# First head pair of a fused attention and two-layer kernel: keys and queries kept whole in float32, bias rows multiplied apart, half of these rows on GpSimd's queue

## The chip, the core and the metric

One core of a Trainium2 chip runs the whole program. The metric is the device time of one execution in microseconds (us), as the median of the runs; lower is better. The core's engines run side by side, each through its own queue in order: TensorE (PE, with its weight loads shown apart as PEld), VectorE (DVE), ScalarE (ACT), GpSimd (POOL) and SyncE (SP), which only issues transfers.

## What is computed

Attention over 4 batches of 8 heads, 576 positions and 64 values a head, with a bias made of running sums, and then two feed-forward layers over all 2304 tokens. Cut to what matters here:

```python
scores = scale * np.matmul(q, k.transpose(0, 1, 3, 2))        # scale = 1/8
cum = np.cumsum(np.maximum(s, 0.0), axis=-1)
bias = -(cum[:, :, :, None] - cum[:, :, None, :])
scores = np.where(causal, -1e9, scores + np.minimum(bias, 0.0))
attn = exp(scores - max(scores)); attn = attn / sum(attn)
x = attn @ v                                                   # then
x = gelu_like(x @ w_in) @ w_out                                # layer 1
out = rational(x @ w2_in) @ w2_out                             # layer 2
```

## The kernel before

Heads go in pairs, four pairs to a batch, sixteen in all. A pair has five **units**, tiles of 128 query rows taken in the order t = 0, 1, 4, 2, 3 (unit 4 holds the last 64 rows of both heads). A unit's scores are made per head h over the n keys that the causal mask leaves: `s_0_2_1` is batch-0 pair 0, unit 2, head 1. In the names of the program's order the last number is only a counter.

**How float32 accuracy is made.** PE takes reduced-precision `float32r` operands in one pass. `prep` turns the keys and queries of a head by PE transposes into PSUM (`tk`, `tq`; `turn`), then splits them: ACT writes a rounded high part (`hi`, L213), DVE writes the rest (`lo`, L216), two ops each of 64 x 288 for a head's keys and as many for its queries. The high parts are then doubled onto the other 64 partitions (`move`; for the first two pairs by GpSimd casts, L251). So a score is two matmuls into one PSUM tile (`scores_piece`, L289): one on 68 partitions (`k2`: low keys with high queries, and in partitions 64 to 67 four **bias rows**, running sums against ones), one on all 128 (`kh`, `qs`).

**Where the bias rows come from.** `sums` makes the running sums in two column parts, `PARTS` = 0 to 256 and 256 to 576 (DVE scan L118), `sum_parts` splits each part into high and low (ACT L129, DVE L130) in the buffer that the trace calls `stgA`, and `open_rows` has SP move them into `k2` (L136): eight transfers for pair 0 (two parts, two heads, two sides), four for pair 1. SP's next transfer after pair 0's eight is the first of the raw weights (L547).

**The loop.** Each step j of `attention` issues the scores of unit j for head 0, then the transposes of the unit three steps back (`tp`, L381; L360 for unit 4), then head 1's scores, then values of older units (`O`, L406). DVE reduces a score tile with its mask and finds the row minimum (L319), ACT takes the exponent (L326), DVE inverts the row sums, GpSimd scales the rows (L339). PE follows the written order; the other engines' order is set by a scheduler. While there is nothing else for PE to do, in the first five steps, `fill` and `warm` put idle bf16 matmuls of 512 columns (L82) between the others: they compute nothing that is used. From step 4 on, ACT, DVE and POOL also convert raw weights (L558 to L567). From the second batch on, layer 1's matmuls of an earlier batch (L638, L662) fill PE's gaps.

Of the kernel before, what the change touches and what calls it, by code (L numbers as in the profile page):

```python
# [10 lines left out]
F32 = mybir.dt.float32  # L11
F32R = mybir.dt.float32r
# [3 lines left out]
AF = mybir.ActivationFunctionType  # L16
ALU = mybir.AluOpType
# [8 lines left out]
NB, NH, S, D = 4, 8, 576, 64  # L26
# [3 lines left out]
P = 128  # L30
# [18 lines left out]
PARTS = ((0, 256), (256, 576))  # L49
ZEROS = 5  # L50
WARM = 6
RUN_ENDS = ((0, 1, 4, 2, 3), (3,), (3,), (3,))
W2_SLOTS = 7
LEAD = 2
# [7 lines left out]
class Fused:  # L62
# [70 lines left out]
    def sum_rows(self, g, src, h=slice(0, 2), c=slice(0, S)):  # L133
        d = self.k2[g % 2][D : D + 4].bitcast(F32)
        for i in range(2):
            self.moved = self.nc.sync.dma_start(d[2 - 2 * i : 4 - 2 * i, i, h, c], src)  # L136

    def open_rows(self, g):
        for c0, c1 in ((0, S),) if g else PARTS:
# [59 lines left out]
    def prep(self, att, b, p, ld, first=False):  # L199
        nc, ident = self.nc, self.ident  # L200
        h0, h1 = slice(0, D), slice(D, P)

        def new(nm):
            return att.tile([P, 2, S], F32R, name=f"{nm}{b}_{p}", tag=nm, bufs=2)

        g = b * NP + p
        kh, qs, k2 = new("kh"), new("qs"), self.k2[g % 2]
        self.pairs[b, p] = {"kh": kh, "qs": qs, "k2": k2, "ld": ld, "O": None}  # L210

        def hi(out, T, scale):
            self.parts[0] = nc.scalar.activation(out, T, AF.Copy, scale=scale)  # L213
# [7 lines left out]
        def turn(nm, h):  # L221
            T = self.bank("T", f"t{nm}{b}_{p}_{h}")
            x = ld[nm][:, h].rearrange("i t d -> i (t d)")
            for t in range(3):
                nc.tensor.transpose(  # L225
                    T[:, t * R6 : (t + 1) * R6], x[:, t * P : (t + 1) * P], ident[:R6, :R6]
                )
            return nm, T[:, : 3 * R6].rearrange("p (t i) -> p i t", i=R6), h

        def split(*parts):  # L230
# [10 lines left out]
            for i, (high, low, T, scale) in enumerate(jobs):  # L241
                with self.behind((self.parts[1],) if i else ()):
                    lo(low, T, high, scale)

        def main(nm):
            split(*[turn(nm, h) for h in range(2)])

        def move(o, i, hs=(0, 1)):
            if g < 2:
                for h in hs:  # L250
                    self.copied = nc.gpsimd.tensor_copy(o[:, h], i[:, h].bitcast(F32))  # L251
            else:
                nc.sync.dma_start(o.bitcast(F32), i.bitcast(F32))

        if first:
            turned = [[turn(nm, h) for nm in "kq"] for h in range(2)]
            for h in range(2):
                with self.behind(first):
                    split(*turned[h])
                first = tuple(self.parts)  # L260
                if h == 0:
                    with self.behind(first):
                        first = self.sum_parts(PARTS[1])
                move(kh[h1], kh[h0], (h,))
                move(k2[h0, 1], qs[h0], (h,))
            self.warm(WARM)
            return
        if g > 1:
            self.sum_rows(g, self.rows[g])
        main("k")  # L270
        move(kh[h1], kh[h0])
        yield
        main("q")
        move(k2[h0, 1], qs[h0])
        yield


# [1 line left out]
    def scores_piece(self, u, sc, hs, j0, w):  # L279
        nc = self.nc  # L280
        b, p, t = u
        pr = self.pairs[b, p]
        for h in hs:
            c0, c1 = t * P, (t + 1) * P
            if t == 4:
                c0, c1 = (S - P if h else S - 64), S
            k2 = pr["k2"][: D + 4]
            for m, (q, k) in enumerate(((k2[:, 1, h], k2[:, 0, h]), (pr["qs"][:, h], pr["kh"][:, h]))):
                nc.tensor.matmul(  # L289
                    sc[: c1 - c0, :w], lhsT=q[:, c0:c1], rhs=k[:, j0 : j0 + w],  # L290
                    start=m == 0, stop=m == 1,
                )

    def unit_scores(self, att, u, h):
# [12 lines left out]
        if t == 4:  # L307
            sc = self.bank("S", f"s{b}_{p}_{t}_{h}")
            j0, w = 288 * h, 288
            self.scores_piece(u, sc, (1, 0), j0, w)  # L310
            mask = self.mask[:, 0:288] if h == 0 else self.mask[:, 640:928]
            i = h
        else:
            sc = self.bank("S", f"s{b}_{p}_{t}_{h}")
            self.scores_piece(u, sc, (h,), 0, max(n, 256))
            j0, w = 0, n
            mask = self.mask[:, 640 - n : 640]
            i = 0
# [17 lines left out]
        rc = nc.vector.reciprocal(inv[:, c], inv[:, c])  # L336
        self.tail = (ex, rc)
        for i, bt in enumerate(bts):
            nc.gpsimd.tensor_scalar(bt[:, :n], bt[:, :n], inv[:, i : i + 1], 1.0, ALU.mult, ALU.mult)  # L339

    def unit_transpose(self, att, u):
        nc, ident = self.nc, self.ident
# [90 lines left out]
    def attention(self, att, mlp):  # L433
# [24 lines left out]
            with self.behind((self.moved,)):  # L458
                self.store_sums()
        opened = self.moved  # L460
        with self.behind((self.copied,)):
            loads[2] = self.pair_load(att, 0, 2, eng=nc.gpsimd)
        later.extend(loads[i]["values"] for i in (1, 2))
        for j in range(n + AHEAD + 1):
            i, k = j - AHEAD, j - AHEAD - 1
            self.zeros = j < ZEROS
# [25 lines left out]
            self.fill(q / 3, j < 4)  # L492
            for _ in tr:
                pass
            if j < n and idx == 4:
                for _ in nprep:
                    pass
                g = b * NP + p
                g = {0: 3, 1: 4, 2: NB * NP}.get(g, g + 2)
                if g < NB * NP:  # L500
                    with self.behind((opened,)):
                        loads[g] = self.pair_load(att, *divmod(g, NP))
                    later.append(loads[g]["values"])
# [506 lines left out]
```

## Time and profile before

| | us |
|---|---|
| median of 3 runs (1021.01, 1022.94, 1023.03) | 1022.94 |
| the profiled execution | 1021.61 |
| its span, first instruction to last | 1019.6 |
| PE busy | 998.2 (98%) |
| DVE, ACT, POOL busy | 797.3, 718.2, 337.8 |

The profiled execution is 2.0 us longer than its span and 1.3 us shorter than the median. Busy shares are means over stages: the opening (about 25 us), the rest of the first batch (to about 90 us), the other three batches (to about 300 us) and the two layers have different limits. In the rows below, a time is us from the start of the span, and the bracket at a row's end is the idle time of its engine just before it, with what ended it.

### The profile page before, as it was taken

Reading aid. Unit: us, or ns where it says so; the run is one execution under the profiler, and the core shown is the slowest. Engines: PE = TensorE matmul, PEld = TensorE weight load, DVE = VectorE, ACT = ScalarE, POOL = GpSimd, SP = SyncE. Lnnn points to the kernel's source line nnn. Section 1 sums busy time; section 2 is a strip of 40 time slices with the busy share of each in tenths; the row PEclk is TensorE's granted clock in tenths of the full one; section 3 lists DMA queues with packets and bytes.
Section 4 is the critical chain, followed back from the end, with each engine's and each line's share of the span. In section 5 each row is a group of like instructions: output and inputs, shape, how many; then the busy total and the mean of one; then the engine's idle time right before and its main releaser. Section 6 shows DMA issues by size and latency. Waiting matters only on the chain.

```text
span 1019.6 us, 19822 instructions
## 1 busy us (share of the span) xinstructions
PE 998.2 (98%) x7053; PEld 933.9 (92%) x7054; DVE 797.3 (78%) x1804; ACT 718.2 (70%) x1661; POOL 337.8 (33%) x503
## 2 busy tenths in 40 slices
PE   7889999999999999999999999999999999999997
PEld 4679999999999999999999999999999999989996
DVE  7897666766537977777778747998988989889886
ACT  5999889878756655555555436787887777777775
POOL 5778656554410012222111112232222222222222
PEclk9999999999999999999999999999999999999999
DMA  7664564543237546776666644010010100100000
GB/s 180 157 175 100 135 188 146 152 123 72 59 125 247 177 140 196 230 235 224 212 189 235 208 133 190 1 31 32 3 60 1 32 32 1 63 1 1 32 1 32
DMA packets 79074, 115.97 MB, mean 114 GB/s; under 512 B 25552, under 2 KB 63072, under 8 KB 77440
## 3 DMA queue, kind: packets, MB, share of 16 engines
q1 hardware_dynamic: 72640, 94.94, 31.4%
q0 software_dynamic: 6112, 19.47, 5.1%
q8 instruction: 56, 0.92, 0.4%
q14 instruction: 42, 0.34, 0.1%
q10 hardware_dynamic: 224, 0.30, 0.1%
HBM read 74.78 MB, written 31.60 MB: 104 GB/s over the span
## 4 chain that ended last, share of the span: by engine, by line
PE 89%; DVE 4%; DMA 3%; ACT 2%; issue 1%; POOL 0%; SPq 0%; ACTq 0%; DVEq 0%
PE h L638 38%; PE a L815 19%; PE a L662 19%; PE s L289 5%; PE O L406 4%; PE tp L381 3%; DMA raw<-in_moe_w_in_dram 1%; DVE bt L319 1%; DMA x2p<-st 1%; DVE k L216 1%; PE tq L225 1%; PE tk L225 1%; ACT bt L326 0%; PE tp L360 0%; DVE qs L216 0%
## 5 line engine op out<-in xcount | busy, mean ns | idle before, releaser
L638 PE MATMUL h<-x,u 128*128 128x288 f32 x1536 | 231.5, 296 | 1.2 <-ACT st L677 1.2
L662 PE MATMUL a<-gh,u 128*128 128x288 f32 x1024 | 231.7, 297 | 0.0
L638 PEld LDWEIGHTS h<-x,u 128*128 128x128 f32 x1536 | 212.8, 188 | 3.1 <-ACT st L677 1.5
L798 POOL TENSOR_TENSOR gl<-u,gh 128x384 fp32r<-128x384 f32 x96 | 105.7, 1101 | 290.4 <-ACT gh L796 266.4
L662 PEld LDWEIGHTS a<-gh,u 128*128 128x128 f32 x1024 | 173.0, 188 | 1.1 <-issue 0.5
L638 PE MATMUL h<-y,u 128*128 128x384 f32 x864 | 165.7, 336 | 0.0
L638 PEld LDWEIGHTS h<-y,u 128*128 128x128 f32 x864 | 152.9, 188 | 6.2
L662 PE MATMUL a<-gl,u 128*128 128x288 f32 x512 | 150.0, 295 | 0.7 <-DVE gl L655 0.7
L815 PE MATMUL a<-u,gh 128*128 128x512 f32 x432 | 114.6, 394 | 0.9 <-ACT gh L796 0.9
L649 ACT ACTIVATE g<-h 128x288 f32<-128x288 f32 x128 | 52.0, 407 | 75.8 <-PE h L638 75.4
L724 POOL DMA_DIRECT2D x<-xp x64 | 35.3, 552 | 207.3 <-DVE g L650 106.7
L662 PEld LDWEIGHTS a<-gl,u 128*128 128x128 f32 x512 | 96.5, 188 | 1.4 <-DVE gl L655 0.9
L326 ACT ACTIVATE bt<-bt,mn 128x128 f32<-128x128 f32 (+2 forms) x144 | 84.1, 585 | 19.3 <-DVE mn L319 18.2
L815 PEld LDWEIGHTS a<-u,gh 128*128 128x128 f32 x432 | 80.0, 188 | 14.9 <-ACT gh L796 1.8
L339 POOL TENSOR_SCALAR bt<-bt,sm 128x128 f32<-128x128 f32 (+2 forms) x144 | 81.7, 579 | 30.0 <-DVE sm L336 21.6
L796 ACT ACTIVATE gh<-u 128x384 fp32r<-128x384 f32 x96 | 50.6, 527 | 57.6 <-DVE u L794 56.6
L319 DVE CUSTOM_DVE_ANT_0 bt<-s,mask 128x128 f32<-128x128 f32 (+2 forms) x144 | 68.9, 482 | 27.6 <-PE s L289 25.5
L652 ACT ACTIVATE gh<-g 128x288 fp32r<-128x288 f32 x128 | 56.5, 442 | 45.6 <-DVE g L650 43.8
L650 DVE SCALAR_TENSOR_TENSOR g<-g,h 128x288 f32<-128x288 f32 x128 | 57.5, 450 | 29.8 <-ACT g L649 29.2
L781 ACT ACTIVATE y<-h,cf 128x384 f32<-128x384 f32 x96 | 55.4, 577 | 33.9 <-PE h L638 33.9
L786 DVE SCALAR_TENSOR_TENSOR y<-s,cf,y 128x384 f32<-128x384 f32 x96 | 59.3, 618 | 20.6 <-ACT s L783 19.3
L794 DVE SCALAR_TENSOR_TENSOR u<-y,u 128x384 f32<-128x384 f32 x96 | 73.5, 765 | 1.1
(116 smaller groups left out, 2048.0 us busy)
## 6 DMA issues: line engine op xcount, KB each, us to landing
raw<-in_moe_w_in_dram SPq DMA_DIRECT2D x24, 512.0 KB
raw<-in_moe_w_out_dram SPq DMA_DIRECT2D x24, 512.0 KB
x<-xp POOLq DMA_DIRECT2D x64, 144.0 KB, 3.0
wd<-park POOLq DMA_DIRECT2D x36, 256.0 KB, 4.3
u<-wd SPq DMA_DIRECT2D x8, 1024.0 KB
x2p<-st SPq DMA_DIRECT2D x32, 144.0 KB
xp<-x2p SPq DMA_DIRECT2D x32, 144.0 KB
xp<-x SPq DMA_DIRECT2D x32, 144.0 KB
```

What stands on the lines that cost most here:

```text
L319: nc.vector.tensor_tensor_reduce(bt[:, j0 : j0 + w], sc[:, :w], mask, 1.0, 3.0e38 if i == 0 else mn[:, 0:1], ALU.add, ALU.min, mn[:, i : i ...
L326: ex = nc.scalar.activation(bt[:, :n], bt[:, :n], AF.Exp, bias=mn[:, i : i + 1], scale=-1.0, accum_out=sm[:, col : col + 1],)
L339: nc.gpsimd.tensor_scalar(bt[:, :n], bt[:, :n], inv[:, i : i + 1], 1.0, ALU.mult, ALU.mult)
L638: nc.tensor.matmul(ps_tile, lhsT=u[:, wl, kk * P : (kk + 1) * P], rhs=x(xl, kk), start=(n == 0), stop=(n == 3 * KD - 1),)
L650: nc.vector.scalar_tensor_tensor(g[:, :w], g[:, :w], 1.0, h, ALU.add, ALU.mult)
L652: self.newest["act"] = nc.scalar.activation(gh[:, :w], g[:, :w], AF.Copy)
L662: nc.tensor.matmul(acc, lhsT=u[:, wl, d * P : (d + 1) * P], rhs=g[gl], start=(first and i == 0), stop=(last and i == 2),)
L781: nc.scalar.activation(y, h, AF.Abs, scale=cf[:, 4:5])
L786: nc.vector.scalar_tensor_tensor(y, s, cf[:, 7:8], y, ALU.mult, ALU.add)
L794: last = nc.vector.scalar_tensor_tensor(p, y, 2.0, p, ALU.subtract, ALU.mult)
L798: nc.gpsimd.tensor_tensor(gl, p, gh.bitcast(F32), ALU.subtract)
L815: nc.tensor.matmul(accs[m], lhsT=g[gl][:, m * P : (m + 1) * P], rhs=u[:, wl, :], start=(f == 0 and i == 0), stop=(f == NF - 1 and i == 2),)
```

## The change

For pair 0 alone (`PLAIN = 1`):

- keys and queries aren't split. `keep` copies them whole, as float32, onto partitions 0 to 63: head 0's keys and queries and head 1's queries by ACT, head 1's keys by DVE. The low parts and the GpSimd doublings of this pair are gone.
- a score is a float32 matmul on 64 partitions and, after it, a `float32r` matmul on partitions 64 to 67 with the bias rows alone. Unit 0 takes its own 128 columns and not 256.
- head 1's four bias-row transfers go to GpSimd's queue, head 0's four stay on SP's.
- the load of pair 2's keys and queries, on GpSimd's queue too, is issued after the first unit's rows are scaled and not ahead of the loop.

```diff
     def sum_rows(self, g, src, h=slice(0, 2), c=slice(0, S)):
         for i in range(2):
-            self.moved = self.nc.sync.dma_start(d[2 - 2 * i : 4 - 2 * i, i, h, c], src)
+            if g == 0 and h == 1:
+                self.nc.gpsimd.dma_start(d[2 - 2 * i : 4 - 2 * i, i, h, c], src)
+            else:
+                self.moved = self.nc.sync.dma_start(d[2 - 2 * i : 4 - 2 * i, i, h, c], src)
...
+        def keep(engs, *parts):
+            done = []
+            for o in range(2):
+                for nm, T, h in parts:
+                    out = (kh if nm == "k" else qs)[h0, h]
+                    out = out.rearrange("p (i t o) -> p o i t", t=3, o=2)[:, o]
+                    src = T[o * D : (o + 1) * D]
+                    scale = 1.0 if nm == "k" else -0.125
+                    if engs[nm] == "act":
+                        done.append(nc.scalar.activation(out, src, AF.Copy, scale=scale))
+                    else:
+                        done.append(nc.vector.tensor_scalar(out, src, scale, None, ALU.mult))
+            return tuple(done)
...
         if first:
             turned = [[turn(nm, h) for nm in "kq"] for h in range(2)]
-            for h in range(2):
-                with self.behind(first):
-                    split(*turned[h])
-                first = tuple(self.parts)
-                if h == 0:
-                    with self.behind(first):
-                        first = self.sum_parts(PARTS[1])
-                move(kh[h1], kh[h0], (h,))
-                move(k2[h0, 1], qs[h0], (h,))
+            opened = keep({"k": "act", "q": "act"}, *turned[0])
+            with self.behind((*opened, *first)):
+                keys = keep({"k": "dve"}, turned[1][0])
+                with self.behind(keys):
+                    opened = self.sum_parts(PARTS[1])
+            with self.behind(opened):
+                keep({"q": "act"}, turned[1][1])
...
-            for m, (q, k) in enumerate(((k2[:, 1, h], k2[:, 0, h]), (pr["qs"][:, h], pr["kh"][:, h]))):
+            terms = ((k2[:, 1, h], k2[:, 0, h]), (qs, kh))
+            if pr["plain"]:
+                terms = ((qs[:D], kh[:D]), (k2[D:, 1, h], k2[D:, 0, h]))
+            for m, (q, k) in enumerate(terms):
...
-            self.scores_piece(u, sc, (h,), 0, max(n, 256))
+            self.scores_piece(u, sc, (h,), 0, n if self.pairs[b, p]["plain"] else max(n, 256))
...
-        with self.behind((self.copied,)):
-            loads[2] = self.pair_load(att, 0, 2, eng=nc.gpsimd)
...
+            if j == 0:
+                with self.behind((self.normed,)):
+                    loads[2] = self.pair_load(att, 0, 2, eng=nc.gpsimd)
```

PE's order keeps its length. At unit 4's head pass and what stands around it (`s_0_4` scores of unit 4, `tq_1` the query transposes of pair 1, `idle` the fillers, `k_0` the tile `k2` with the bias rows), before:

```order
L82 MATMUL idle<-mask 128x512
L289 MATMUL s_0_4_0_285<-k_0_134 128x288
L289 MATMUL s_0_4_0_285<-kh_0_150,qs_0_151 128x288
L289 MATMUL s_0_4_0_285<-k_0_134 64x288
L289 MATMUL s_0_4_0_285<-kh_0_150,qs_0_151 64x288
L225 MATMUL tq_1_0_291<-ident,spare 128x96 x3
```

and PE's order at the same place now:

```order
L83 MATMUL idle<-mask 128x512
L316 MATMUL s_0_4_0_273<-kh_0_150,qs_0_151 128x288
L316 MATMUL s_0_4_0_273<-k_0_134 128x288
L316 MATMUL s_0_4_0_273<-kh_0_150,qs_0_151 64x288
L316 MATMUL s_0_4_0_273<-k_0_134 64x288
L231 MATMUL tq_1_0_279<-ident,spare 128x96 x3
```

The two matmuls of a piece have changed places, the first is now float32 on 64 partitions and the second has four partitions; the fillers and transposes stand where they stood.

DVE's order in the opening, from the second part of the running sums (L118) to the first score reduction (L319), before:

```order
L118 SCALAR_TENSOR_TENSOR cum<-s_114,cum,nz 32x320
L216 SCALAR_TENSOR_TENSOR k_0_134<-tk_0_0_152,kh_0_150 64x288
L216 SCALAR_TENSOR_TENSOR qs_0_151<-tq_0_0_156,qs_0_151 64x288
...
L130 TENSOR_TENSOR stgA<-cum,stgA 32x320
L216 SCALAR_TENSOR_TENSOR k_0_134<-tk_0_1_160,kh_0_150 64x288
L216 SCALAR_TENSOR_TENSOR qs_0_151<-tq_0_1_164,qs_0_151 64x288
...
L319 ISA bt_0_0_0_216,mn_0_0_0_217<-s_0_0_0_218,mask 128x128
```

and DVE's order there now:

```order
L119 SCALAR_TENSOR_TENSOR cum<-s_114,cum,nz 32x320
L262 TENSOR_SCALAR kh_0_150<-tk_0_1_160 64x288 x2
L131 TENSOR_TENSOR stgA<-cum,stgA 32x320
L346 ISA bt_0_0_0_200,mn_0_0_0_201<-s_0_0_0_202,mask 128x128
```

Eight low parts (four on either side of the sums' second part) have become two copies, and the first reduction follows the sums directly.

GpSimd's order after its masks, before:

```order
L251 CAST kh_0_150<-kh_0_150 64x576
L251 CAST k_0_134<-qs_0_151 64x576
L251 CAST kh_0_150<-kh_0_150 64x576
L251 CAST k_0_134<-qs_0_151 64x576
L181 DMA kn_2_211<-in_k_dram 96x2x384
L181 DMA qn_2_213<-in_q_dram 96x2x384
L339 TENSOR_SCALAR bt_0_0_0_216<-bt_0_0_0_216,sm_0_0_215 128x128
```

and GpSimd's order there now:

```order
L138 DMA k_0_134<-stgA 2x1x256 x2
L138 DMA k_0_134<-stgA 2x1x320 x2
L366 TENSOR_SCALAR bt_0_0_0_200<-bt_0_0_0_200,sm_0_0_199 128x128
L366 TENSOR_SCALAR bt_0_0_1_211<-bt_0_0_1_211,sm_0_0_199 128x128
L185 DMA kn_2_223<-in_k_dram 96x2x384
L185 DMA qn_2_225<-in_q_dram 96x2x384
```

Four casts are replaced by four small transfers, and the load for pair 2 stands behind the first unit's scaling. On ACT, six copies take the place of eight. Further on in the first batch the scheduler has moved some of ACT's and POOL's weight conversions by one to three places.

## Rows read from the trace of the kernel before

**Rows 1.** Busy time by stretch: stretch, its length, busy us (instructions) of each engine, clock.

```profile
16.00:21.70 5.70, 5.67 (x35) 4.10 (x36) 5.03 (x17) 2.95 (x9) 3.09 (x6) 1.00 0.70 152
...
25.00:90.00 65.00, 58.10 (x543) 47.13 (x540) 58.24 (x196) 63.79 (x182) 49.62 (x77) 1.00 0.62 160
90.00:300.00 210.00, 209.06 (x2058) 201.99 (x2057) 129.50 (x441) 169.60 (x486) 112.15 (x198) 1.00 0.42 113
```

**Rows 2.** Chain that ended last, in the opening: start, us, what.

```profile
11.94 3.96 DMA k<-stgA
```

**Rows 3.** Timeline of the opening: start, us, engine, line, operation, out<-in.

```profile
9.16 0.95 DVE L130 TENSOR_TENSOR stgA<-cum,stgA 32x320 fp32r<-32x320 f32 x1
...
9.83 0.81 POOL L251 CAST k<-qs 64x576 fp32r<-64x576 f32 x1
...
11.55 0.46 DVE L216 SCALAR_TENSOR_TENSOR qs<-tq,qs 64x288 fp32r<-64x288 f32 x1
...
12.05 0.29 DVE L319 CUSTOM_DVE_ANT_0 bt<-s,mask 128x128 f32<-128x128 f32 x1
```

**Rows 4.** Timeline of the opening, PE's matmuls.

```profile
9.29 0.36 PE L289 MATMUL s<-k 68*128 68x256 f32 x1 [1.02 <-DMA k<-stgA]
...
16.24 0.29 PE L289 MATMUL s<-kh,qs 128*128 128x288 f32 x1
...
16.37 0.30 PE L289 MATMUL s<-k 68*64 68x288 f32 x1
...
16.64 0.66 PE L225 MATMUL tq<-ident,spare 96*128 96x96 f32 x6
...
17.91 0.61 PE L82 MATMUL idle<-mask 128*128 128x512 bf16 x2
...
18.71 0.39 PE L82 MATMUL idle<-mask 128*128 128x512 bf16 x1
...
20.66 0.60 PE L381 MATMUL tp<-ident,bt 128*128 128x128 f32 x4
...
21.34 0.40 PE L289 MATMUL s<-kh,qs 128*128 128x512 f32 x1
```

**Rows 5.** PE's groups by shape over the whole run: count, busy us, mean ns.

```profile
L406 PE MATMUL O<-pt,vn 128*64 128x128 f32 x640 | 43.3, 277 | 0.0
L289 PE MATMUL s<-kh,qs 128*128 128x512 f32 x32 | 12.8, 400 | 0.0
L406 PE MATMUL O<-pt,vn 128*64 128x64 f32 x320 | 12.2, 223 | 0.0
L289 PE MATMUL s<-kh,qs 128*128 128x288 f32 x32 | 9.5, 297 | 0.0
```

**Rows 6.** Timeline of PE around one block of float32 value matmuls.

```profile
150.23 0.34 PE L289 MATMUL s<-kh,qs 128*128 128x384 f32 x1
150.50 2.99 PE L406 MATMUL O<-pt,vn 128*64 128x128 f32 x60
153.42 0.50 PE L289 MATMUL s<-k 68*128 68x512 f32 x1
```

**Rows 7.** Timeline where the opening ends: DVE's and ACT's last steps for unit 3.

```profile
23.18 0.67 DVE L319 CUSTOM_DVE_ANT_0 bt<-s,mask 128x512 f32<-128x512 f32 x1
...
24.14 0.72 ACT L326 ACTIVATE bt<-bt,mn 128x512 f32<-128x512 f32 x1
...
24.86 0.66 ACT L558 ACTIVATE stgA<-stgA 128x512 int32<-128x512 uint32 x1
```

**Rows 8.** Transfers: two timeline rows, and one of issues with us to landing.

```profile
6.00 6.50 SPq L136 DMA_DIRECT2D k<-stgA  x8
...
10.59 0.84 POOL L181 DMA_DIRECT2D kn<-in_k_dram  x1
...
kn<-in_k_dram POOLq DMA_DIRECT2D x1, 288.0 KB, 3.9
```

More of the change, by code (lines that the diff above doesn't have):

```diff
@@ L51 @@
 WARM = 6
+PLAIN = 1
 RUN_ENDS = ((0, 1, 4, 2, 3), (3,), (3,), (3,))
@@ L201, in prep @@
         h0, h1 = slice(0, D), slice(D, P)
+        g = b * NP + p
+        plain = g < PLAIN
         def new(nm):
-            return att.tile([P, 2, S], F32R, name=f"{nm}{b}_{p}", tag=nm, bufs=2)
-        g = b * NP + p
+            return att.tile(
+                [P, 2, S], F32 if plain else F32R, name=f"{nm}{b}_{p}", tag=nm, bufs=2
+            )
         kh, qs, k2 = new("kh"), new("qs"), self.k2[g % 2]
-        self.pairs[b, p] = {"kh": kh, "qs": qs, "k2": k2, "ld": ld, "O": None}
+        self.pairs[b, p] = {"kh": kh, "qs": qs, "k2": k2, "ld": ld, "O": None, "plain": plain}
         def hi(out, T, scale):
@@ L243, in split @@
                     lo(low, T, high, scale)
-        def main(nm):
-            split(*[turn(nm, h) for h in range(2)])
+        def keep(engs, *parts):
[11 more added lines that the diff above has]
+            return tuple(done)
+        def main(nm):
+            parts = [turn(nm, h) for h in range(2)]
+            if plain:
+                keep({"k": "act", "q": "dve"}, *parts)
+            else:
+                split(*parts)
         def move(o, i, hs=(0, 1)):
@@ L250, in move @@
                 for h in hs:
-                    self.copied = nc.gpsimd.tensor_copy(o[:, h], i[:, h].bitcast(F32))
+                    nc.gpsimd.tensor_copy(o[:, h], i[:, h].bitcast(F32))
             else:
@@ L270, in prep @@
         main("k")
-        move(kh[h1], kh[h0])
+        if not plain:
+            move(kh[h1], kh[h0])
         yield
         main("q")
-        move(k2[h0, 1], qs[h0])
+        if not plain:
+            move(k2[h0, 1], qs[h0])
         yield
@@ L286, in scores_piece @@
                 c0, c1 = (S - P if h else S - 64), S
[L287 to L288 removed]
+            k2, qs, kh = pr["k2"][: D + 4], pr["qs"][:, h], pr["kh"][:, h]
+            terms = ((k2[:, 1, h], k2[:, 0, h]), (qs, kh))
+            if pr["plain"]:
+                terms = ((qs[:D], kh[:D]), (k2[D:, 1, h], k2[D:, 0, h]))
+            for m, (q, k) in enumerate(terms):
                 nc.tensor.matmul(
@@ L338, in unit_scores @@
         for i, bt in enumerate(bts):
-            nc.gpsimd.tensor_scalar(bt[:, :n], bt[:, :n], inv[:, i : i + 1], 1.0, ALU.mult, ALU.mult)
+            self.normed = nc.gpsimd.tensor_scalar(
+                bt[:, :n], bt[:, :n], inv[:, i : i + 1], 1.0, ALU.mult, ALU.mult
+            )
     def unit_transpose(self, att, u):
@@ L460, in attention @@
         opened = self.moved
-        with self.behind((self.copied,)):
-            loads[2] = self.pair_load(att, 0, 2, eng=nc.gpsimd)
-        later.extend(loads[i]["values"] for i in (1, 2))
+        later.append(loads[1]["values"])
         for j in range(n + AHEAD + 1):
@@ L494, in attention @@
                 pass
+            if j == 0:
+                with self.behind((self.normed,)):
+                    loads[2] = self.pair_load(att, 0, 2, eng=nc.gpsimd)
+                later.append(loads[2]["values"])
             if j < n and idx == 4:
```

## The prediction

> **What bounds the kernel now.** I began with the busy time by stretch. From 90 us on PE is busy for 209.06 of 210.00 us, and behind that its work is fixed, so a shift of the moment at which that stretch begins is carried to the end one for one. Ahead of it, from 25 to 90 us, ACT is the fullest engine, 63.79 of 65.00 us [rows 1]: it has 1.21 us of idle time, so a later start there can win back 1.21 us at most. Its work in this stretch isn't touched by the change (pair 0 is split before it; the scheduler only swaps neighbours). So the question is when ACT comes to the end of the opening. I take as marker the last exponent of pair 0's unit 3, which starts at 24.14, right ahead of the first weight conversion at 24.86; it follows DVE's last reduction of pair 0, at 23.18 [rows 7].
>
> What holds the opening before? Not PE: its last score matmul of pair 0 ends at 21.34 + 0.40 = 21.74 [rows 4], 1.4 us ahead of the reduction that reads it. It is DVE and a transfer. DVE writes low parts until 11.55 + 0.46 = 12.01 and only then, at 12.05, reduces its first tile [rows 3]. And the sums' second part, from 9.16, is ready only at 10.11 [rows 3], behind four low parts, so that the last bias rows, issued at 11.94, land at 15.90 [rows 2]; unit 4's scores wait for them. Yet in the stretch from 16.00 to 21.70 PE is busy for 5.67 of 5.70 us [rows 1], fillers included. PE has no room where the change gives it more to do. That decides the case.
>
> **What is removed.** DVE has two copies in place of eight low parts of some 0.46 us: 6 x 0.46 = 2.8 us less. It reaches the sums' second part two steps earlier, at about 8.2, and ends it by 9.2 at the latest (0.95 for that op, during part of which GpSimd's casts run [rows 3]; the casts are gone). ACT has six copies for eight; GpSimd loses four casts, the last from 9.83. All of this lies ahead of the first score or beside it. The first score's gate stays: PE waited until 9.29 for head 0's bias rows [rows 4], and the two transfers that bring them still go out first on SP, from 6.00 [rows 8]. What is late next is PE.
>
> **What PE gets to do.** I add up PE's stream from 9.29 to the end of unit 3's scores, by streaming time, not by record length (records overlap).
> - Float32: the value matmuls are float32, 480 of them in the program and 640 + 320 = 960 records, so two records each. A record of 128 columns takes 277 ns and one of 64 takes 223 [rows 5]: 54 ns for 64 columns, 0.84 ns a column, 1.69 ns for a float32 matmul of two records. A `float32r` matmul goes from 297 to 400 ns between 288 and 512 columns: 0.46 ns a column [rows 5].
> - Pair 0 behind its first score has 11 pieces (unit 0 one, unit 1 two, unit 4 four, units 2 and 3 two each) of 128, 2 x 256, 4 x 288, 2 x 384 and 2 x 512 columns, 3584 together. Float32: 3584 x 1.69 = 6.1 us. Bias rows: 3584 x 0.46 = 1.6 us. Before, two matmuls at 0.46 made 3.4 us of them (unit 0 with 256 columns).
> - Unchanged: 16 fillers, of which one alone lasts 0.39 and two 0.61, so 0.22 us each, 3.5 us; 12 transposes of pair 1, single float32 records of 96 columns at 0.84, 0.08 each, 1.0; 6 transposes of exponents of 128 columns, 0.11 each, 0.7 (six of the first kind last 0.66, four of the second 0.60: that many streams and the tail of the last record) [rows 4].
> Sum: 6.1 + 1.6 + 3.5 + 1.0 + 0.7 = 12.9. From 9.29 + 0.06 the stream ends at 22.2, and the result can be read some 0.15 later, at 22.4. So without any wait PE is just where DVE wants it: 22.4 against 23.18.
>
> **The changes of mode.** PE now goes from bf16 or transposes to float32 on 64 partitions, to `float32r` on 4, and back, 11 times. The trace has no such sequence; the nearest are the float32 value blocks [rows 6]. The score matmul ahead of one ends at 150.57, the one behind it at 153.92. In these 3.35 us lie 2.69 us of value streams (40 records of 128 and 20 of 64 columns at 0.84, two heads at once on the two halves of the columns) and 0.23 us of the score behind. So 0.43 us go to entering and leaving. Leaving alone is 153.92 - 153.49 - 0.23 = 0.20; of the other 0.23 some is the small cost of sixty records, and I take half, 0.11. Price of a piece: 0.31, between 0.20 and 0.43. Zero is possible too: from 128 to 64 columns wide, score matmuls follow each other at 16.24 and 16.37, 0.13 us apart, their streaming time [rows 4], so a narrower tile by itself costs nothing. I take 0.31, since the value blocks are float32 as the new scores are. 11 x 0.31 = 3.4: the last score can be read at 22.4 + 3.4 = 25.8.
>
> **The sum.** DVE's reduction at 25.8 and not at 23.18, ACT's exponent 0.67 later, at 26.4 to 26.5 and not at 24.14: 2.3 us late. Half of ACT's 1.21 us of idle time is waiting that a late ACT no longer meets: 0.6 back. That leaves 1.7 us. The profiled execution would go from 1021.61 to 1023.3; it stood 1.3 below the median, and against the median of 1022.94 I say 1024.6.
>
> **What I cost at nothing.** Head 1's rows on GpSimd's queue: an issue there took 0.84 and a landing 3.9 us [rows 8], both for 288 KB and not for 2 KB. The first two, from 6.0, land by 6.0 + 0.84 + 3.9 = 10.7; PE wants them at about 10.6. The last starts by 9.2 + 0.84, lands by 13.9; PE comes to unit 4 at 14 with the mode changes and at 13 without, so the cover is PE itself, and up to 0.9 us would show if there are none. On SP eight issues took 6.50 us [rows 8], now four: the raw weights start 2 to 3 us earlier, and ACT wants them only after 24. The load for pair 2 goes out behind the first scaling, at about 13, and lands by 19; its transposes stand behind the last score of unit 3. GpSimd's casts for pair 1 queue behind it, 1.5 us, and are wanted at 22 or later.
>
> **The rivals.**
> *No price for the changes (A).* Then PE's last score is read at 22.4, reduced by 23.1, and the exponent starts at 23.1 against 24.14: 1.0 us gained, 1021.9. If the bias matmul, on partitions of its own, also runs beside the float32 one, PE is 1.6 earlier still, but DVE is then the bound (four reductions, the pair-1 low parts and small ops between), and I give it 0.4 more: 1021.5. For it: the 0.13 us at 16.37 [rows 4]. Against it: the 0.20 at 153.49 [rows 6].
> *Each piece pays three changes (B), the side of slower.* If leaving the four-partition matmul costs the 0.20 of rows 6 again, a piece costs 0.51, 11 of them 5.6 us, 2.2 more than I forecast: 1026.8. It decides (over 2.05 us slower) from 0.34 us a piece. For it: the bias matmul lies on another set of rows than what follows. The Trainium skill has a rule that speaks for this: "TensorEngine Tiling (Array Packing)", Key Properties, says that changing the tiling mode drains TensorE, and that tiles work in parallel within a mode. By that rule all three steps of a piece would be changes, 64 rows, the bias rows' own, 128 rows, and the time would be the 1026.8 above; the trace agrees at 153.42 and doesn't at 16.37.
> *GpSimd's rows come late (C).* If small transfers on that queue need over 5 us, unit 4 waits with all behind it; a landing at 16 would cost 2 us more than the forecast: 1026.6. The 3.9 us of a load of 288 KB speak against it.
> *It doesn't do what it says:* the built order shows the matmuls, the copies and the queue as described, so this has no chance of its own.
>
> **How the numbers follow.** Forecast 0.52 (its own range 1023.4 to 1026, from 0.20 and 0.43 a piece), A 0.29, B 0.13, C 0.06. A measurement of this kernel can tell 0.2%, 2.05 us, from no change: 1020.9 to 1025.0. A third of the forecast lies above 1025.0, with all of B and most of C: slower 0.35. Faster needs A with the overlap and luck in the order of the first batch: 0.08. Same: 0.57. The range takes in A and the middle of B: 1021.3 to 1026.8.
>
> **What would show it.** In the changed profile: float32 score records two to a piece, at 0.84 ns a column; gaps of 0.1 to 0.2 us around them; DVE's last reduction of pair 0 waiting for PE near 25.8 (near 22.4 for A, near 28 for B), and ACT idle ahead of the first conversion. The prediction is wrong if fillers give way, if PE isn't what the reductions wait for behind unit 4, or if the first batch's new order moves ACT's stretch by more than a microsecond.

## The result, and the profile after

The changed kernel takes 1034.95 us (median of six runs, 1030.37 to 1042.88) against 1022.45 (six runs of the kernel before beside it): 1.0132 times as long, 95% interval 1.009 to 1.0174. By the medians it is slower by 12.5 us, far outside the range that was forecast (1021.3 to 1026.8). Its profiled execution took 1038.77 us, its span 1036.9.

The page of the changed kernel, TensorE's busy share of the span in part 1 and the granted clock in part 2 (40 slices of 26 us, tenths of full speed). The kernel before had 9 in every slice.

```profile
PE 1018.9 (98%) x7065; PEld 941.7 (91%) x7066; DVE 796.9 (77%) x1798; ACT 719.3 (69%) x1659; POOL 335.0 (32%) x503
...
PEclk8798999999999999999999999999999999999999
```

The first, second and fourth slice are below 9. By stretch (the columns are those of [rows 1]; the clock stands behind POOL), the changed kernel:

```profile
16.00:19.00 3.00, 3.00 (x16) 1.40 (x14) 1.97 (x7) 1.23 (x6) 2.12 (x5) 1.00 0.96 254
19.00:22.00 3.00, 3.00 (x8) 0.89 (x8) 2.18 (x6) 0.78 (x3) 1.44 (x3) 0.54 1.11 280
...
28.00:31.00 3.00, 3.00 (x5) 0.92 (x5) 0.20 (x2) 0.59 (x2) 0.00 (x0) 0.50 0.00 0
...
37.00:40.00 3.00, 3.00 (x19) 2.34 (x18) 2.23 (x7) 2.61 (x9) 1.56 (x2) 0.55 0.31 101
```

From 19 us on the clock is at its lower level, 1.2 GHz (0.50), up to about 39 us. TensorE is busy for 3.00 of 3.00 us ahead of the fall and all through it: no idle stretch lies right ahead of the fall. The last long one, 1.41 us, ends at 9.86. [rows 1] had 1.00 in this place.

Timeline of TensorE in the changed kernel (L316 the scores, L83 the fillers), the answer to [rows 4]:

```profile
9.86 0.29 PE L316 MATMUL s<-k 4*128 4x128 f32 x1 [1.41 <-DMA k<-stgA]
...
15.52 0.75 PE L316 MATMUL s<-kh,qs 64*128 64x288 f32 x2
16.20 0.39 PE L316 MATMUL s<-k 4*128 4x288 f32 x1
16.52 0.69 PE L316 MATMUL s<-kh,qs 64*64 64x288 f32 x2
17.15 0.34 PE L316 MATMUL s<-k 4*64 4x288 f32 x1
17.42 0.71 PE L231 MATMUL tq<-ident,spare 96*128 96x96 f32 x6
...
21.84 1.65 PE L316 MATMUL s<-kh,qs 64*128 64x384 f32 x2
...
32.26 2.07 PE L316 MATMUL s<-kh,qs 64*128 64x512 f32 x2
34.26 0.79 PE L316 MATMUL s<-k 4*128 4x512 f32 x1
```

Up to 19 us the opening runs ahead of the old one: unit 4's scores start at 15.52, where they had waited until 16.03 for the last bias rows. Then a float32 piece of 384 columns lasts 1.65 us, and the last bias product of pair 0 starts at 34.26. DVE's last reduction starts at 35.09; ACT's exponent, the forecast's marker ([rows 7]: 24.14), and the first conversion behind it (24.86) are now here:

```profile
35.88 0.72 ACT L353 ACTIVATE bt<-bt,mn 128x512 f32<-128x512 f32 x1 [2.22 <-DVE mn L346]
36.60 0.66 ACT L589 ACTIVATE stgA<-stgA 128x512 int32<-128x512 uint32 x1
```

The marker is 11.74 us late. The rest of this execution's loss (it took 17.16 us more than the one before) arises behind it, in part from two further falls, each behind a gap of TensorE (78 to 80 us is the other). One-microsecond stretches of the changed kernel:

```profile
57.00:58.00 1.00, 0.00 (x0) 0.00 (x0) 1.00 (x3) 0.99 (x5) 0.00 (x0) 1.00 0.46 107
...
60.00:61.00 1.00, 1.00 (x10) 0.80 (x10) 0.99 (x4) 1.00 (x3) 0.65 (x3) 0.59 0.94 178
61.00:62.00 1.00, 1.00 (x11) 0.67 (x8) 0.97 (x4) 0.62 (x2) 0.94 (x1) 0.50 0.82 307
```

The transfers did as forecast. Issues of GpSimd's queue in the opening, with us to landing:

```profile
k<-stgA POOLq DMA_DIRECT2D x2, 2.0 KB, 2.8
...
k<-stgA POOLq DMA_DIRECT2D x2, 2.5 KB, 1.6
```

### The profile page after: what moved, and what is told of

Read it like the earlier page. It is cut to its first block, busy times and chain, and to the rows that moved or that the text cites. A ratio compares the mean times of both kernels' runs of the same rounds, so it can differ in the third digit from the quotient of the medians.

```text
span 1036.9 us, 19845 instructions
## 1 busy us (share of the span) xinstructions
PE 1018.9 (98%) x7065; PEld 941.7 (91%) x7066; DVE 796.9 (77%) x1798; ACT 719.3 (69%) x1659; POOL 335.0 (32%) x503
## 4 chain that ended last, share of the span: by engine, by line
PE 89%; DVE 4%; DMA 2%; ACT 1%; issue 1%; POOL 1%; SPq 0%; ACTq 0%; DVEq 0%; POOLq 0%
PE h L669 37%; PE a L846 19%; PE a L693 18%; PE s L316 6%; PE O L435 4%; PE tp L410 3%; DMA raw<-in_moe_w_in_dram 1%; DVE bt L346 1%; PE tk L231 1%; DMA x2p<-st 1%; PE tp L389 1%; PE tq L231 1%; PE idle L83 1%; DVE k L222 0%; DVE stgA L594 0%
## 5 line engine op out<-in xcount | busy, mean ns | idle before, releaser
L316 PE MATMUL s<-k 68*128 68x256 f32 (+5 forms) x192 | 73.4, 386 | 1.4 <-DMA k<-stgA 1.4
```

The costliest lines, as they stand in the source:

```text
L316: nc.tensor.matmul(sc[: c1 - c0, :w], lhsT=q[:, c0:c1], rhs=k[:, j0 : j0 + w], start=m == 0, stop=m == 1,)
```

## The experiments

**Theory 1** is what the trace after suggests: the new stream of products (64 and 4 rows of the array instead of 128 and 68) keeps TensorE busy in the records, but does not hold its clock. The expectations split it: is it float32 and the changes of mode (1b, F, M), the narrow operands (1a, N, N4), or idle waits? The rival to all of them was my own forecast: the price of the changes of mode alone.

To place the runs, one table from the traces: where ACT starts the last exponent of pair 0, the first and the ninth weight conversion, in the profiled execution of each kernel, and the median time of all its runs.

| kernel | exponent | 1st conversion | 9th | median us |
|---|---|---|---|---|
| before | 24.14 | 24.86 | 93.33 | 1022.5 to 1023.2 |
| after | 35.88 | 36.60 | 111.21 | 1034.95 |
| e1 double fill | 32.29 | 33.01 | 102.13 | 1030.85 |
| e2 one product | 26.37 | 27.10 | 97.88 | 1026.02 |
| e5 float32r narrow | 30.06 | 30.79 | 103.78 | 1032.97 |
| e7 bias on 68 | 28.33 | 29.05 | 100.26 | 1028.71 |
| e9 one product, held | 24.75 | 25.47 | 97.91 | 1025.93 |
| e10 fewer fillers | 22.39 | 23.11 | 95.60 | 1023.49 |
| e12 gap filled | 22.66 | 23.38 | 94.44 | 1023.21 |

**e1: twice the fillers.** In the changed kernel's `fill`, while pair 0 opens:

```diff
-            self.warm(warm if self.zeros else 0)
+            self.warm(2 * warm if self.zeros else 0)
```

> The changed kernel with twice the idle matmuls in the first five steps (32 for 16 behind the first score). Theory 1, TensorE's clock falls at 19.4 us because its stream there is too thin (64- and 4-partition matmuls with gaps between): twice the fillers hold the granted clock at 1.00 through the opening, PE's last score of pair 0 comes at about 22.4 + 11 x 0.33 + 3.5 = 29.5 us, the exponent behind it at 30 and not at 35.88, and the time is about 1029. Theory 2, float32 products by themselves lower the clock whatever stands between them: it falls as before, the fillers add 3.5 us at full and 7 at half clock, and the time is 1039 or more.

Measured: 1030.85 us (1030.03 to 1032.03), 1.0075 times before's [1.006, 1.009]. More work on the engine that is full, and 4 us less time. In e1's trace the clock is 1.00 throughout, and the piece that took 1.65 us above takes 0.91. Two rows of e1's timeline, TensorE and the marker on ACT:

```profile
23.32 0.91 PE L316 MATMUL s<-kh,qs 64*128 64x384 f32 x2
...
32.29 0.72 ACT L353 ACTIVATE bt<-bt,mn 128x512 f32<-128x512 f32 x1 [1.08 <-DVE mn L346]
```

So the fillers hold the clock, and the fall is what costs most. The marker came 2.3 us later than I expected: the start, the pieces and the fillers all took more than I had put in. The idle stretch at the start is the same as in the changed kernel (1.42 us, up to 9.86), so that it alone does not bring the fall.

**e2: one product.** The opening pair's bias rows stand as partitions 64 to 67 under its float32 keys and queries, and go there by the same queues; a piece is one product on 68 partitions.

```diff
...
-                terms = ((qs[:D], kh[:D]), (k2[D:, 1, h], k2[D:, 0, h]))
+                terms = ((qs[: D + 4], kh[: D + 4]),)
...
```

> The changed kernel with the bias rows as partitions 64 to 67 of the float32 operands: one float32 matmul on 68 partitions a piece, no bias matmul of its own, one change of mode in and one out. Theory 1a, the thin part is the 4-partition matmul and the gaps around it: without it the clock stays at 1.00, PE's last score comes at 22.4 - 1.6 + 11 x 0.2 to 0.31 = 23 to 24.2, and the time is 1022 to 1024. Theory 1b, the float32 product on half the partitions is what is too thin: the clock falls as before (0.50 for some 15 us) and the time is 1030 or more.

Measured: 1026.02 us, 1.0029 [1.0018, 1.004]. One more memset on DVE and one on GpSimd stand ahead of the sums, and the first score waited until 11.71 for its bias rows (1.83 us). Behind that wait the clock fell, but under the new products it came back, and stayed at 1.00 for the rest of the opening. e2 by stretch:

```profile
13.00:16.00 3.00, 3.00 (x13) 2.29 (x12) 0.98 (x6) 0.81 (x5) 0.00 (x0) 0.50 0.60 183
16.00:19.00 3.00, 3.00 (x17) 1.85 (x17) 1.73 (x6) 2.44 (x9) 2.86 (x6) 0.97 0.70 114
19.00:22.00 3.00, 2.94 (x14) 1.57 (x13) 2.88 (x10) 1.37 (x4) 2.22 (x5) 1.00 1.01 247
```

**e3: the bias product on 68 rows.** The changed kernel with 64 rows of zeros above the four bias rows, so that the second product is 68 rows wide:

```diff
...
-                terms = ((qs[:D], kh[:D]), (k2[D:, 1, h], k2[D:, 0, h]))
+                terms = ((qs[:D], kh[:D]), (k2[:, 1, h], k2[:, 0, h]))
```

> The changed kernel, but the bias matmul takes 68 partitions, zeros in 64 of them, so that it runs as wide as the fillers; its columns and the count of matmuls are unchanged. If a piece's gaps come from the tile of the bias rows, the piece gets shorter than 0.33 us beyond its streams; if they come from float32, it stays. Theory 1a: the clock stays at 1.00, 1025. Theory 1b or 2: it falls as in the changed kernel, 1035.

Measured: 1041.85 us, 1.0183 [1.0166, 1.02], worse than the change. Not a clean test: writing the zeros held back the bias rows, TensorE waited for them, and the clock was at 0.50 right behind that wait. e3's first bias product, and a later stretch:

```profile
11.36 0.45 PE L318 MATMUL s<-k 68*128 68x128 f32 x1 [2.31 <-DMA k<-stgA]
```

```profile
13.00:16.00 3.00, 3.00 (x8) 1.45 (x7) 0.47 (x3) 0.49 (x2) 0.00 (x0) 0.50 0.64 181
```

**e4: the transfers alone.** The kernel before, with head 1's bias rows on GpSimd's queue and pair 2's load behind the first scaling, as in the change.

> The kernel before with the part of the change that concerns transfers alone: head 1's four bias-row transfers of pair 0 on GpSimd's queue, pair 2's load behind the first scaling. Both theories: the clock stays at 1.00. The last bias rows land at about 13.5 and not at 15.90, so unit 4's scores start 1 to 2 us earlier; DVE is the bound from there, so 0 to 1.5 us are gained: 1021 to 1022.5.

Measured: 1023.94 us, 1.0009 [1.0, 1.0019]. The rows did come earlier (unit 4's scores started at 14.73, not at 16.03), but it brought nothing: in 22 to 28 us TensorE was busy for 3.44 of 6.00 us, and behind that the clock was at 0.64 (28 to 34).

**e5: narrow, but float32r.** The changed kernel with the unsplit keys and queries in `float32r`; the low halves are left out, and unit 0 takes 256 columns again.

```diff
-                [P, 2, S], F32 if plain else F32R, name=f"{nm}{b}_{p}", tag=nm, bufs=2
+                [P, 2, S], F32R, name=f"{nm}{b}_{p}", tag=nm, bufs=2
...
```

> The change with one thing altered: the opening pair's unsplit keys and queries are held as float32r instead of float32, so that its scores are a float32r product on 64 partitions and a float32r product on 4 partitions, with no float32 matmul and no change of mode in between, and at least 256 columns as before. What it leaves out: the low halves of that pair's keys and queries, so their rounding stays in the scores. Fillers and everything else are those of the change. Theory N (the products are too narrow: 64 and 4 of the array's rows hold the clock less than 128 and 68 did): the granted clock falls here too, to 0.5-0.6 somewhere between 18 and 40 us, and the time is 1028-1036. Theory F (it is float32 with its changes of mode, not the narrow operands): the clock stays at 1.00 through the opening, the exponent of unit 3 starts near 22.5-23.5 (24.14 in the kernel before, 1.75 us of earlier rows less the two-filler stream that is unchanged), and the time is 1020.5-1022.5.

Measured: 1032.97 us, 1.0103 [1.007, 1.0137]. No float32 score is left, and the clock falls even earlier. e5 by stretch, and two pieces of 256 columns ahead of the fall:

```profile
13.00:16.00 3.00, 3.00 (x15) 1.38 (x12) 2.02 (x9) 2.41 (x8) 2.19 (x5) 0.96 0.57 103
16.00:19.00 3.00, 3.00 (x11) 1.75 (x10) 1.97 (x7) 1.57 (x4) 1.95 (x4) 0.50 1.03 241
```

```profile
12.09 0.38 PE L316 MATMUL s<-kh,qs 64*128 64x256 f32 x1
12.41 0.38 PE L316 MATMUL s<-k 4*128 4x256 f32 x1
12.71 0.71 PE L231 MATMUL tk<-ident,spare 96*128 96x96 f32 x6
```

Theory F falls, N stands: narrow products are enough. The rows show something more. From 64 rows to 4 and on takes 0.32 and 0.30 us, where two `float32r` products of 256 columns on 68 and 128 rows take 0.12 each (12.97, 13.09 and 13.21 in e8, below). So leaving a narrow product costs some 0.19 us also where both are `float32r`.

**e6: one product, rows early.** e2 with as many memsets ahead of the sums as the change has.

> The one-product kernel again (the bias rows stand as partitions 64 to 67 under the opening pair's float32 keys and queries, so each piece of a score is one float32 product on 68 partitions), now with as many memsets ahead of the sums as the change itself has, so that the bias rows land near 9.9 us and not at 11.7. Theory 1a (the four-row product and the changes of mode round it let the clock fall; the float32 product on 64 to 68 partitions does not): the granted clock is 1.00 from 10 to 40 us, the exponent of unit 3 starts at 23-24.6, and the time is 1020.5-1023.5. Theory 1b (any float32 product in this stream lets it fall): the clock falls to 0.5 at 19-20 us as in the change, the exponent is near 33-35, the time 1031-1036.

Measured: 1022.61 us (ten runs), 1.0003 [0.9981, 1.0025]. Nine runs lie between 1021.04 and 1025.47, one at 1031.56, and the profile caught that one: TensorE stood idle for its bias rows, and the clock was at 0.74 in 10 to 13 us and at 0.50 until 34. e6's first score:

```profile
9.85 0.46 PE L326 MATMUL s<-kh,qs 68*128 68x128 f32 x2 [2.22 <-DMA qs<-stgA]
```

**e7: the bias product on 68 rows, rows early.** e3 with the zeros written by DVE and GpSimd behind the first rows' transfers.

> The widened bias product again (float32 product on 64 partitions, then the float32r bias product on 68 partitions, of which 64 are zeros), now with the zeros written behind the bias rows' first transfers, so that the rows land near 9.9 us and not at 11.4. Theory N4 (it is the product on 4 partitions that lets the clock fall): the clock is 1.00 through the opening, every piece costs 0.31-0.38 us over its streams as in the change at full clock, the exponent of unit 3 starts near 26, the time is 1023.5-1026. Theory M (it is the two kinds of matmul in turn, float32 and float32r, with a stop between them, whatever the width): the clock falls to 0.5 between 15 and 20 us, the exponent starts past 33 and the time is 1031-1042.

Measured: 1028.71 us (1027.83 to 1029.11), 1.0054 [1.0033, 1.0075]. This is the cleanest pair: in the code only the zero rows and their writing differ from the changed kernel, and 6.2 us and most of the spread are gone. e7's clock is 1.00 up to 34 us. That is more than one profile: the mean clock of e7's four executions is 0.995 to 0.998, of e1's four 0.999 to 1.00, of the changed kernel's six 0.980 to 0.995. One stretch; then two pieces, with the transposes behind them:

```profile
19.00:22.00 3.00, 3.00 (x12) 1.22 (x11) 2.35 (x7) 1.01 (x3) 1.56 (x3) 1.00 1.09 280
```

```profile
15.48 0.75 PE L320 MATMUL s<-kh,qs 64*128 64x288 f32 x2
16.16 0.40 PE L320 MATMUL s<-k 68*128 68x288 f32 x1
16.49 0.70 PE L320 MATMUL s<-kh,qs 64*64 64x288 f32 x2
17.11 0.35 PE L320 MATMUL s<-k 68*64 68x288 f32 x1
17.30 0.66 PE L234 MATMUL tq<-ident,spare 96*128 96x96 f32 x6
```

Theory N4 had the clock right; its time, 1023.5 to 1026, was too low, and so was its marker (26; measured 28.33).

**e8: before without fillers** (`ZEROS = 0`, so that the sixteen fillers behind the first score are gone).

> The kernel before with no fillers after the first score (its sixteen filler matmuls among the opening pair's scores are left out; the opening's own fillers ahead of the first score stay). This tells whether the split float32r scores need the fillers for their clock. Theory 1 (a thin stream lets the clock fall, and before's scores at 128 and 68 partitions are only a little thicker than the change's): the granted clock falls to 0.5-0.8 between 15 and 40 us, and what the 16 fillers took (about 4.9 us of TensorE at 0.30) is more than lost: 1024-1032. Rival (before's scores hold the clock by themselves; float32 and narrow products alone lose it): 1.00 throughout, the exponent of unit 3 starts 1-4 us earlier than 24.14, time 1019-1022.5.

Measured: 1024.99 us, 1.0019 [1.0007, 1.0031]. The old scores need the fillers too: with the fillers gone TensorE waits for longer (1.79 us up to 15.97), the clock falls, and what the fillers took is more than lost. But it recovers by itself, the marker is only 0.80 us late (24.94). e8 by stretch, and the two products of 256 columns mentioned under e5:

```profile
16.00:19.00 3.00, 3.00 (x14) 2.92 (x15) 2.05 (x8) 1.59 (x5) 1.07 (x2) 0.50 0.73 185
19.00:22.00 3.00, 3.00 (x15) 2.64 (x14) 2.73 (x7) 1.31 (x4) 2.19 (x4) 0.70 0.77 170
```

```profile
12.97 0.28 PE L289 MATMUL s<-k 68*128 68x256 f32 x1
13.09 0.28 PE L289 MATMUL s<-kh,qs 128*128 128x256 f32 x1
13.21 0.66 PE L225 MATMUL tk<-ident,spare 96*128 96x96 f32 x6
```

**e9, e10, e11.** e9 is e6 with `WARM = 13` for 6; e10 is e9 without four fillers, the last one of each of the first four steps; e11 is e5 with the zero rows of e7.

> The one-product kernel whose bias rows land early, with seven more fillers (13, not 6) ahead of the first score. In the profile of that kernel without them TensorE waited idle from 7.63 to 9.85 us for the bias rows, and the clock fell right behind that wait (0.74 in 10 to 13, 0.50 to 34) in a run of 1031.56, where its other nine runs lie at 1021.0 to 1025.5. Theory 1a (68-partition float32 products hold the clock, and the idle wait ahead of them was what lost it): the clock is 1.00 from 6 to 40 us, no run is above 1026, the exponent of unit 3 starts at 23.5-25, the median is 1020.5-1023. Theory 1b (the single float32 products lose the clock now and then by themselves): falls to 0.5 between 10 and 34 us in some runs again, and the spread of the ten or so runs stays near 10 us.

> The kernel of the run before with four of the sixteen fillers among the scores left out (those behind each unit's second score of the first four steps). A filler takes 0.21 to 0.30 us of TensorE at full clock, so that four are worth 0.8 to 1.2 us where TensorE is the bound. If the 68-partition float32 products hold the clock with fewer fillers: exponent of unit 3 at 22.5-24, median 1019.8-1022. If the fillers are what holds it: the clock falls to 0.5 between 13 and 30 us and the median is 1024-1032.

> The float32r kernel with narrow products again (opening pair's keys and queries rounded to float32r, so that their low halves are left out), but with the bias product on 68 partitions, of which 64 are zeros: the scores are a float32r product on 64 partitions and one on 68. With 64 and 4 partitions the clock fell to 0.50 from 16 us on. Theory N4 (the product on 4 partitions is what loses the clock): 1.00 through the opening, each piece of 288 columns takes about 0.35 us less of stops than at 64 and 4, the exponent of unit 3 starts at 23-24.5, time 1020.5-1024. Theory N64 (64 partitions in float32r are too narrow as well): the clock falls between 15 and 22 us and the time is 1027-1036.

Measured, e9: 1025.93 us, 1.0028 [1.0017, 1.0039], twelve runs from 1022.78 to 1027.85. In its profile the clock holds up to 31 us (0.50 in 31 to 34, behind 1.59 busy of 3.00), so the spread of 10 us is gone, but the thirteen fillers took 4.42 us there and the first score started only at 11.82 (10.08 in e10). Inconclusive on the time. e10: 1023.49 us, 1.0004 [0.9992, 1.0016], twelve runs from 1019.72 to 1025.13. With four fillers fewer the clock held through the opening; the marker is 1.75 us earlier than before's. Three runs had a mean clock of 1.00 (1019.72, 1020.08 and 1022.14); the other nine had 0.995 to 0.997 (1022.51 to 1025.13). e10's clock falls behind a gap at the end of the opening:

```profile
27.00:28.00 1.00, 0.00 (x0) 0.00 (x0) 0.99 (x4) 0.96 (x4) 0.91 (x2) 1.00 0.76 169
28.00:29.00 1.00, 0.93 (x13) 0.79 (x14) 0.97 (x5) 0.82 (x2) 0.92 (x2) 0.79 0.73 161
29.00:30.00 1.00, 1.00 (x17) 0.88 (x16) 0.97 (x4) 0.68 (x3) 1.00 (x3) 0.50 0.68 144
```

e11: 1029.62 us, 1.0059 [1.004, 1.0078]; one run of four at 1024.93 with a clock of 0.997, three near 1029.8 at 0.987 or 0.988. In the profile, one of the three, the clock was at 0.87 in 10 to 13 and at 0.50 from 13 to 34 us, behind a wait of 1.64 us for DVE's zeros, so that N4 and N64 are not told apart by it. The fourth run, at 0.997, can't have had such a fall; that speaks for N4, but it left no trace.

**e12 and e13: fillers in the gap.** Twelve fillers more, two after each score of the three steps behind the opening: e12 in e10, e13, the control, in the kernel before.

```diff
-ZEROS = 5
+ZEROS = 8
...
-            self.fill(q / 3, 1 if j else 4)
+            self.fill(q / 3, 4 if j == 0 else 1 if j < 5 else 2)
...
-            self.fill(q / 3, j < 4)
+            self.fill(q / 3, 1 if j < 4 else 0 if j < 5 else 2)
```

> The one-product kernel with fewer fillers (exponent of unit 3 at 22.39, 1.75 us ahead of the kernel before; median 1023.49, two of twelve runs at 1019.7 and 1020.1 with a clock of 1.00, the rest at 0.995 to 0.997), with twelve fillers added where TensorE stood idle behind the opening: two after each score of the three steps behind it (unit 0 to unit 4 of pair 1, about 22 to 30 us). Theory G (the gain of the earlier opening is given back because the clock falls behind TensorE's gap of 25 to 28 us): the clock stays at 1.00 from 22 to 40 us, the median comes to 1019.7-1021.5 and the spread narrows. Rival (the pipeline behind the opening is bound by the vector engines and the loads, so that an earlier opening is lost there whatever the clock): the clock holds but the median stays at 1022-1024.

> Control: the same twelve fillers in the same three steps of the kernel before, whose opening is as it was. Theory G: before's own runs differ by the same falls (clock 0.995 to 1.000, 1021.4 to 1024.7), so that its median comes down to 1021-1022.3 and its spread narrows, and it stays 1 to 2 us behind the one-product kernel with the same fillers. Rival: no change, or up to 1.5 us slower where the fillers stand in the way of TensorE (12 x 0.21 to 0.26 = 2.5 to 3.1 us of its time, against 2.0 us idle in 22 to 28).

Measured, e12: 1023.21 us, 1.0003 [0.9994, 1.0012], 1021.35 to 1024.73. e13: 1024.73 us, 1.0021 [1.001, 1.0032]. Theory G's time did not come: in e12's profile the clock is 1.00 in every stretch, the marker is 1.48 us early, and the execution took 1022.37 all the same. That does not clear the falls. Not all of e12's runs held the clock: four had a mean of 1.00 (1021.35 to 1022.78), seven 0.997 or 0.998 (1023.20 to 1024.73); e10's runs part in the same way. And in e12 DVE has another order. DVE of e12 (L602 to L604 belong to the weight conversion, L400 copies pair 0's exponents), and TensorE waiting for that copy:

```profile
24.64 0.43 DVE L602 TENSOR_SCALAR stgA<-stgA 128x512 f32<-128x512 f32 x1 [0.76 <-ACT stgA L601]
25.10 0.80 DVE L603 TENSOR_SCALAR stgA<-stgA 128x512 int32<-128x512 int32 x1
25.94 0.69 DVE L604 SCALAR_TENSOR_TENSOR stgA<-stgA 128x512 int32<-128x512 int32 x1
26.55 0.68 DVE L400 COPY pt<-tp 128x512 f32<-128x512 f32 x1
```

```profile
27.29 1.03 PE L237 MATMUL tq<-ident,qn 96*128 96x96 f32 x6 [1.63 <-DVE pt L400]
```

In the kernel before the same copy stands behind the first of these three and starts at 26.45. Here it stands behind the third and starts at 26.55, so that the lead is gone at this one step; by the ninth conversion e12 is 1.11 us behind. In e12 the earlier opening is lost in the order of DVE's work behind it, with the clock at its full level.

e10 has the old order at this place (its copy starts at 24.70, 1.75 us early) and loses its lead elsewhere. Its third weight conversion still starts 1.07 us ahead of the old one; then TensorE waits 1.98 us for DVE (up to 45.49), the clock is at 0.50 from 46 to 49 us, and the fourth is 0.37 us late (49.56 against 49.19). The third conversion before and in e10, and e10's stretch behind it:

```profile
40.96 0.68 ACT L558 ACTIVATE stgA<-stgA 128x512 int32<-128x512 uint32 x1
...
39.89 0.67 ACT L599 ACTIVATE stgA<-stgA 128x512 int32<-128x512 uint32 x1
...
40.00:50.00 10.00, 8.02 (x73) 6.79 (x69) 7.77 (x27) 9.28 (x26) 8.22 (x13) 0.83 0.57 154
```

e13 is 2.0 us slower by the medians with these fillers, its falls included, and the old opening is not safe either: in its profiled execution (1026.34) the clock was at 0.71 in 10 to 13 us, behind a wait of 1.64 us for GpSimd. Whether e10 would be faster with its own order and the clock held in every run was not tried; its three runs at 1.00 are too few to tell.

## Why the prediction was wrong

- **The step that failed: no term for TensorE's clock.** The sum took every duration from a stretch at 1.00 and put a change of the clock at nothing, without a reason. TensorE was busier than before, and the clock fell at 19 us: 11.74 us at the marker, where e7 at full clock has 4.19. Widening the four-row product to 68 rows (e7) holds it through the opening and takes back 6.2 of the 12.5 us (medians); twice the fillers (e1) hold it too; narrow `float32r` products (e5) lose it. So narrow second products lose the clock in this stream, and wide ones hold it. Not shown is whether the width itself does it or the pauses that narrow products leave. From the first bias product to unit 4's scores for head 1 the changed kernel takes 8.42 us (9.86 to 18.28) and e7 7.90 (10.21 to 18.11) for the same columns, and of this difference the records show at most 0.16 us as idle. Whether the 4 rows alone do it, or 64 and 4 together, is open too (e11).
- **Which rule bears on it.** The Trainium skill, "TensorE: Matmul & The Clock Gate", section "HAM oscillation — how this bites in real kernels", has the clock fall where TensorE waits for data; e3, e6 and e10 agree with it, behind waits of 2.31 and 2.22 us and behind the empty microsecond from 27. The fall at 19 us in the changed kernel does not look like that kind: 3.00 of 3.00 us busy on both sides of it, and e1 has the same wait 9 us earlier without a fall.
- **The sum at full clock was 1.8 us short.** e7 gives it, start to start. Its pieces, from the first bias product on, take 11.2 us (forecast 11.2), its transposes 1.8 (1.7), its sixteen fillers 4.2 (3.5), and it begins at 10.21, not at 9.29: 10.21 + 17.2 = 27.4 for the end of the stream, against 25.6. The fillers' term was mis-sized because I took their own time: one filler ahead of a piece on 64 rows takes 0.31 us from start to start (13.78 to 14.09), ahead of e10's piece on 68 rows 0.22 (12.61 to 12.83). In the changed kernel the first bias product started at 9.86: it, not the float32 one, waits for the transfer, 0.57 us later than in [rows 4].
- **The price of a piece was right.** Two pieces of 288 columns in the changed kernel, 15.52 to 17.42, take 1.90 us; their streams are 2 x 288 x (1.69 + 0.46) ns = 1.24, so 0.33 each at full clock, forecast 0.31. 1.69 ns a column is exact: in e10 the one product of 512 columns takes 0.86 us from start to start (18.85 to 19.71). Rival A, no price, and rival B, 0.51, both fall. B's mechanism is there all the same: e5 shows 0.19 us behind each narrow product without any change of type. The Trainium skill, "TensorEngine Tiling (Array Packing)", section "Key Properties", says that changing the tiling mode drains TensorE; that agrees with e5's 0.32 and 0.30 against 0.12.
- **Rival C fell:** small transfers on GpSimd's queue landed after 2.8 and 1.6 us. So what I cost at nothing shows no cost, unless the 0.57 us at the start are its doing (no run parts them), and unit 4's wait did go. e4 shows no gain from this half of the change alone.
- **"One for one" holds for delays, not for a lead.** e1, at full clock throughout, is 8.15 us late at the marker, 8.80 at the ninth conversion and 7.7 in the median. But a lead of 1.48 (e12) or 1.75 us (e10) is gone by then, in e12 by the order of DVE's work, in e10 behind a wait and a fall of the clock. "ACT wins back 0.6" did not happen either: ACT's stretch is not its own work alone, it depends on the order in which DVE, ACT and TensorE meet, and on the clock behind every gap.
- **The rest of the change's loss.** e7's 5.7 us over the kernel before begin with the 4.19 us at its marker; behind it lies a fall (0.68 in 34 to 37 us, behind 0.87 busy of 3.00). The 6.2 us between e7 and the changed kernel are not the clock of the opening alone, because the scheduler gave ACT another order in the first batch. In the changed kernel four copies of queries stand ahead of the fifth weight conversion, before and in e7 behind it:

```profile
70.07 1.53 ACT L219 ACTIVATE qs<-tq 64x288 fp32r<-64x288 f32 x4
...
71.86 0.67 ACT L589 ACTIVATE stgA<-stgA 128x512 int32<-128x512 uint32 x1
```

From the fourth conversion to the fifth it takes 9.25 us, against 6.72 before and 6.69 in e7, and the next step gives 1.25 of these back. So the new order moved ACT's stretch by 1.3 us, one of the signs of being wrong that the prediction names; it had taken it that only neighbours are swapped. The profiled run's falls at 60 and 81 us may be why it lies above the median; the other runs left no trace.

By the medians none of the kernels beats the one before: e6, e10 and e12 come to within 0.04% of it.

## What to carry to other kernels

Put a line for the clock into the sum whenever a change makes TensorE's operands narrower, even where the engine is as busy as before: look for the nearest stretch with such operands, and if there is none, say that the clock is unknown and give both levels' times. Filler matmuls are part of a stream: before the products beside them are changed, ask what the fillers were holding up. And a lead won ahead of a scheduled pipeline counts only as far as the next place where the order of an engine, or a gap and the fall of the clock behind it, gives it back; follow the marker through two or three more steps before it is carried to the end.

## What the runs showed of the hardware that was not expected

- TensorE's clock went from 1.00 to 0.50 with no idle time in the records for the 3 us ahead of it, under products on 64 and 4 partitions (19 us, and 16 us in e5), and stayed at 1.00 under the same float32 products with the other product on 68 (e7).
- Products that follow one on 4 or 64 partitions start some 0.19 us late, `float32r` behind `float32r` (e5 against e8).
- At the start of the program the granted clock reads 1.00 in rows that run slower than that: in e9 thirteen fillers took 4.42 us, 0.34 each, in e10 2.97, 0.23 each, with 1.00 in both from 6 to 10 us. That column is to be read beside the durations there.
